# Seven idle products, an earlier load of the cap, and a layer norm shared out anew among three engines

## The chip, the core and the metric

The kernel runs on one NeuronCore of a Trainium2 chip. Five engines work side by side, each through its own queue in program order: TensorE (PE, with its weight loads PEld), VectorE (DVE), ScalarE (ACT), GpSimd (POOL), and SyncE (SP), which only issues transfers here. An instruction that waits holds up everything behind it on its engine. The metric is the device time of one execution in microseconds (us); the median of three runs is given, beside one execution that was profiled.

## What is computed

Attention with a capped score, then a Fourier mixing over tokens and features, a layer norm without weights, and a feed-forward block; four batches, 12 heads of 64, 448 tokens, all in f32:

```python
scores = cap * tanh((q @ k.T / 8) / cap)                 # cap is a scalar input, 30.0
attn = exp(scores - max); attn = attn / (sum(attn) + 1e-9)
x = (attn @ v) with the heads side by side               # (4, 448, 768)
u = x + real(fft(fft(x, axis=1), axis=2))
un = (u - mean(u)) / sqrt(var(u) + 1e-6)                 # over the 768 features
out = u + relu(un @ w_ch1) @ w_ch2                       # 768 -> 3072 -> 768
```

## The kernel before

**Stages.** Scores are made in tiles t = 0, 1, 2, ... of two heads and up to 128 keys: `scores` writes 2 x 450 columns to one of two PSUM buffers with four products, one for each quarter of the array (line 376). ScalarE turns them into `a` with tanh (386, scale `tscale`) and exp in place (389, scale `capt`). `weigh` multiplies them with v (405) into one PSUM buffer `av`, for a pair of heads, with a column of ones for the row sums. `denominators` (420, 421) adds `guard`, the place of 1e-9, and takes the reciprocal; `normalise` (427) writes the pair's part of `u` and so frees `av` for the next pair. When a batch has its six pairs, the mixing follows (446 to 529), then the norm.

**The norm of a batch b.** `moments` leaves mean and variance of every token in `stat`: 113 rows by 4 groups of tokens. `rows` makes scale and bias of every token from them, on GpSimd: ten operations on 128x4 values, among them a power of -0.5 (549) and one step of Newton's method to sharpen it. `rows_cols` (561) turns mean and deviation into two rows by a product with the identity, for a later addition; `rows_copy` (567) and `rows_out` bring them to memory. `standardise` (582) scales and shifts `u` in place, four operations of 113x768 on VectorE. `u_cols` (589) transposes the result, `u_copy` (297, as `xc<-pt`) fetches it from PSUM, `operand` and `operand_rest` split it into a high and a low part (`xs`, 297 and 302).

**Feed-forward.** The weights come as 64-bit numbers and are split by VectorE and ScalarE (`wt`, 636 to 670). `product` calls `up` (`ph`, 723; ScalarE's relu 734; VectorE's rest 735) and `down` (`po`, 752; VectorE's accumulation 761). The first products fill places between the attention and the norms; after about 260 us the products run in a row to the end.

**What sets the order.** Every step is a function that is put in a plan with `at(f, ...)`. Its place is a number from the table `ORDER`, one list per function; the plan is sorted by these numbers and run inside `tc.manual_schedule()`. The queues hold what a step issues, in that order but for small moves by the framework's scheduler, which puts an instruction where it reckons its inputs to be there.

**What the change touches.** `load_cap` and `scales` with their numbers in `ORDER`, the head of the program before the plan, `rows`, `rows_cols` and `standardise`.

Of the kernel before, what the change touches and what calls it, by code (L numbers as in the profile page):

```python
# [11 lines left out]
F32 = mybir.dt.float32  # L12
# [105 lines left out]
    "load_cap": [  # L118
        4
# [144 lines left out]
def attention_fft_ffn(  # L264
# [44 lines left out]
    nc.scalar.activation(guard, mhalf[:, :1], AF.Tanh)  # L309

# [8 lines left out]
    def load_cap():  # L319
        nc.sync.dma_start(capt, cap.partition_broadcast(P))  # L320

    def scales():
        nc.vector.reciprocal(tscale, capt)
        nc.vector.tensor_scalar_mul(tscale, tscale, 1.0 / math.sqrt(D))


        nc.vector.tensor_scalar_mul(ncap, capt, -1.0)
        nc.vector.tensor_tensor(ncap, ncap, capt, op=ALU.min)
        nc.scalar.activation(guard, ncap, AF.Exp)
        nc.vector.tensor_scalar_mul(guard, guard, 1e-9)  # L330
# [210 lines left out]
    def rows(b):  # L541


        ln = line[b] = new([P, 2, 4, 2], F32, "ln", 2, "ln")
        var = new([P, 4], F32, "var", 1, "var")
        t = new([P, 4], F32, "nt", 1, "nt")
        nc.gpsimd.tensor_copy(ln[:, 0, :, 0], stat[b][:, :, 0])
        nc.gpsimd.tensor_scalar_add(var, stat[b][:, :, 1], 1e-6)
        nc.gpsimd.tensor_tensor(ln[:, 1, :, 0], var, mhalf, op=ALU.pow)  # L549
        nc.gpsimd.tensor_tensor(t, ln[:, 1, :, 0], ln[:, 1, :, 0], op=mul)  # L550
        nc.gpsimd.tensor_tensor(t, t, var, op=mul)
        nc.gpsimd.tensor_scalar(t, t, -0.5, 1.5, op0=mul, op1=add)
        nc.gpsimd.tensor_tensor(ln[:, 1, :, 0], ln[:, 1, :, 0], t, op=mul)
        nc.gpsimd.tensor_tensor(ln[:, 0, :, 1], ln[:, 1, :, 0], var, op=mul)
        nc.gpsimd.tensor_tensor(t, ln[:, 0, :, 0], ln[:, 1, :, 0], op=mul)
        nc.gpsimd.tensor_scalar_mul(ln[:, 1, :, 1], t, -1.0)

    def rows_cols(b):
# [3 lines left out]
            ps[:8, :R], line[b][:R, 0].rearrange("q g a -> q (g a)"), ident[:R, :R], start=True, stop=True  # L562
# [16 lines left out]
    def standardise(b, g):  # L579
        u, ln = u_t[b][:R, g], line[b]  # L580
        scale, bias = ln[:R, 1, g, :1], ln[:R, 1, g, 1:]
        nc.vector.tensor_scalar(u, u, scale, bias, op0=mul, op1=add)
# [222 lines left out]
    at(load_cap)  # L805
    at(scales, needs=[("load_cap",)])
# [17 lines left out]
    def attend(t):  # L824
# [6 lines left out]
        for p in range(B * NP):  # L831
            if 7 * p + 6 in (2 * t, 2 * t + 1):
                at(denominators, p, needs=[("weigh", 7 * p + 6)] + ([("denominators", p - 1)] if p else []))
# [148 lines left out]
```

## Time and profile before

| | |
|---|---|
| median of 3 runs | 934.06 us (934.03 to 934.49) |
| the profiled execution | 935.5 us |
| its span, first to last instruction | 933.4 us |
| busy: PE, PEld | 914.4, 790.5 us (98%, 85%) |
| busy: DVE, ACT, POOL | 715.6, 325.9, 16.7 us (77%, 35%, 2%) |
| chain of waits, by engine | PE 86%, ACT 8%, DVE 3%, POOL 1%, issue 1% |

The profile is of one execution. The chain of waits follows the work that ended last back to what released it, step by step; idle time of an engine that is not on it costs nothing. Three quarters of it are the products of lines 723 and 752. The change stands in the first quarter of the span, so the rows that follow are of the start and of the four norms: GpSimd's rows of batches 0 to 3 begin at 84.8, 135.0, 189.1 and 231.6 us.

### The profile page before, as it was taken

How to read it: one execution, taken by the hardware profiler on the slowest of the kernel's cores; microseconds unless marked ns; L12 is line 12 of the kernel's file. 1: busy time of each engine (PE TensorE's matmuls, PEld its weight loads, DVE VectorE, ACT ScalarE, POOL GpSimd, SP SyncE). 2: the span in 40 equal slices, each digit the busy share in tenths (PEclk: the TensorE clock that was granted, in tenths of full speed). 3: DMA queues.
4: the chain of work that ended last, by engine and by line, in shares of the span. 5: the costliest groups of instructions: out<-in, count | busy, mean ns of one | idle time of the engine just before them, and what ended most of it. 6: DMA issues, size and time to landing. Idle time of an engine off the chain costs nothing.

```text
span 933.4 us, 18643 instructions
## 1 busy us (share of the span) xinstructions
PE 914.4 (98%) x7816; PEld 790.5 (85%) x7816; DVE 715.6 (77%) x1446; ACT 325.9 (35%) x499; POOL 16.7 (2%) x47
## 2 busy tenths in 40 slices
PE   7999999989999999999999999999999999999998
PEld 4666776668889999999998999999999999999997
DVE  2689798879989787878878778777787777778633
ACT  7989989851312222122121221222122221222200
POOL 0001010010100000000000000000000000000000
PEclk9999999989999999999999999999999999999999
DMA  6654435210203121221211121211222111221033
GB/s 184 170 154 136 129 90 129 65 38 1 79 0 85 52 61 51 61 65 54 61 51 61 52 64 47 60 51 51 54 55 63 51 51 51 53 67 51 18 119 118
DMA packets 50467, 66.63 MB, mean 71 GB/s; under 512 B 25552, under 2 KB 36560, under 8 KB 50384
## 3 DMA queue, kind: packets, MB, share of 16 engines
q1 hardware_dynamic: 50240, 65.22, 24.6%
q8 instruction: 61, 1.00, 0.4%
q10 hardware_dynamic: 144, 0.23, 0.1%
q14 instruction: 22, 0.18, 0.1%
HBM read 59.91 MB, written 5.52 MB: 70 GB/s over the span
## 4 chain that ended last, share of the span: by engine, by line
PE 86%; ACT 8%; DVE 3%; issue 1%; POOL 1%; DMA 0%; POOLq 0%; DVEq 0%
PE ph L723 37%; PE po L752 37%; PE av L405 5%; PE s L376 4%; ACT a L389 4%; ACT a L386 4%; PE yps L477 1%; PE pq L505 1%; PE pt L589 1%; DVE bs L538 0%; DMA q<-qr 0%; POOL ln L549 0%; DVE hh L735 0%; DVE xc L761 0%; DVE y L497 0%
## 5 line engine op out<-in xcount | busy, mean ns | idle before, releaser
L752 PE MATMUL po<-hh,w 128*128 128x448 f32 x1728 | 362.4, 367 | 2.0 <-DVE xc L761 1.6
L723 PE MATMUL ph<-xs,w 128*128 128x448 f32 x1728 | 360.1, 367 | 0.0
L752 PEld LDWEIGHTS po<-hh,w 128*128 128x128 f32 x1728 | 322.6, 188 | 34.2 <-DVE xc L761 4.5
L723 PEld LDWEIGHTS ph<-xs,w 128*128 128x128 f32 x1728 | 324.1, 188 | 28.6 <-issue 0.4
L761 DVE TENSOR_TENSOR xc<-xc,po 128x448 f32<-128x448 f32 x288 | 176.1, 617 | 43.0 <-PE po L752 42.7
L735 DVE SCALAR_TENSOR_TENSOR hh<-ph,hh 128x448 fp32r<-128x448 f32 x96 | 59.9, 624 | 97.0 <-ACT hh L734 96.9
L636 ACT ACTIVATE wt<-raw 128x384 f32<-128x384 f32 x84 | 46.6, 555 | 231.1 <-DVE w L670 231.1
L734 ACT ACTIVATE hh<-ph 128x448 fp32r<-128x448 f32 x96 | 52.3, 545 | 191.8 <-PE ph L723 191.8
L405 PEld LDWEIGHTS av<-vt,a 128*64 128x64 f32 (+3 forms) x3072 | 88.2, 133 | 30.1 <-issue 19.0
L405 PE MATMUL av<-vt,a 128*64 128x65 f32 (+3 forms) x3072 | 94.3, 225 | 4.3 <-issue 3.4
L389 ACT ACTIVATE a<-a,capt 128x900 f32<-128x900 f32 x84 | 85.3, 1043 | 1.4
L386 ACT ACTIVATE a<-s,tscale 128x900 f32<-128x900 f32 x84 | 82.5, 1002 | 9.5 <-PE s L376 9.1
L297 ACT CAST w<-wt 128x384 fp32r<-128x384 f32 x84 | 42.8, 510 | 119.2 <-DVE wt L645 119.2
L376 PE MATMUL s<-q,k 64*64 64x450 f32 x672 | 78.0, 563 | 5.9 <-DMA q<-qr 4.7
L645 DVE SCALAR_TENSOR_TENSOR wt<-wt 128x384 f32<-128x384 f32 x96 | 53.6, 559 | 9.5 <-DVE wt L642 0.5
L642 DVE SCALAR_TENSOR_TENSOR wt<-raw,wt 128x384 uint32<-128x384 uint32 x96 | 53.7, 559 | 3.3
L670 DVE TENSOR_TENSOR w<-wt 128x384 fp32r<-128x384 f32 x96 | 53.6, 558 | 3.3
L664 DVE SCALAR_TENSOR_TENSOR wt<-raw,wt 128x384 f32<-128x384 uint32 x96 | 53.5, 558 | 2.9
L302 DVE TENSOR_TENSOR wt<-wt,w 128x384 f32<-128x384 f32 x96 | 52.8, 550 | 0.0
L376 PEld LDWEIGHTS s<-q,k 64*64 64x64 f32 x672 | 20.2, 135 | 27.9 <-ACT a L386 12.1
L639 DVE TENSOR_SCALAR wt<-raw 128x384 uint32<-128x384 uint32 x96 | 34.1, 355 | 1.1
L661 DVE TENSOR_SCALAR wt<-wt 128x384 uint32<-128x384 uint32 x96 | 34.0, 354 | 0.6
(58 smaller groups left out, 323.9 us busy)
## 6 DMA issues: line engine op xcount, KB each, us to landing
raw<-w2r SPq DMA_DIRECT2D x48, 384.0 KB, 4.1
raw<-w1r SPq DMA_DIRECT2D x48, 384.0 KB, 3.0
q<-qr SPq DMA_DIRECT2D x35, 225.0 KB, 4.3
outT<-xc SPq DMA_DIRECT2D x24, 224.0 KB, 1.9
k<-kr SPq DMA_DIRECT2D x12, 256.0 KB, 3.5
vt<-vr SPq DMA_DIRECT2D x24, 128.0 KB, 4.5
k<-kr SPq DMA_DIRECT2D x12, 192.0 KB, 2.4
vt<-vr SPq DMA_DIRECT2D x24, 96.0 KB, 4.1
```

The source lines that it names most:

```text
L376: nc.tensor.matmul(ps_t[t][h * D : (h + 1) * D, n, :SQ], kt[q, k][rows, k0, h], qk[q, x][rows], start=True, stop=True,)
L386: nc.scalar.activation(a_t[t], ps_t.pop(t)[:, :, :SQ], AF.Tanh, scale=tscale)
L389: nc.scalar.activation(a_t[t], a_t[t], AF.Exp, scale=capt)
L405: nc.tensor.matmul(pa_t[p][q0:q1, j, g * (D + 1) : (g + 1) * (D + 1)], a_t[t][rows, n, OFF[g] + q0 : OFF[g] + q1], vt[rows, p % 2, i], sta ...
L642: nc.vector.scalar_tensor_tensor(tu, hi.bitcast(U32), 0xC0000000, tu, op0=ALU.bitwise_and, op1=ALU.bitwise_or)
L645: nc.vector.scalar_tensor_tensor(t, w, HI_MIN, t, op0=ALU.is_ge, op1=mul)
L664: nc.vector.scalar_tensor_tensor(w, lo, 2.0**-52, w, op0=mul, op1=mul)
L670: nc.vector.tensor_tensor(ws[c][1][:, sl], t, w, op=add)
L723: nc.tensor.matmul(ph[:, :S], w_[:, dc * P : (dc + 1) * P], x_, start=(k_ == 0), stop=(k_ == 3 * NDC - 1),)
L735: nc.vector.scalar_tensor_tensor(hh[:, 1], ph[:, :S], 0.0, f32(hh[:, 0]), op0=ALU.max, op1=sub)
L752: nc.tensor.matmul(po[:, :S], w_[:, dc * P : (dc + 1) * P], hh[:, x_], start=(k_ == 0), stop=(k_ == 3 * GF - 1),)
L761: nc.vector.tensor_tensor(ac, ac, po[:, :S], op=add)
```

## The change

- Ahead of the plan, in a scheduled block of its own, seven products of the identity with itself into a PSUM buffer that nobody reads, and behind them the load of the cap. `load_cap` is no longer a step.
- `scales` keeps the two operations for `tscale`. The four for `guard` (one of them an exp on ScalarE) are a step `guards`, number 13, which the denominators need.
- `rows`: GpSimd adds 1e-6 and takes the power. VectorE does six operations: three for Newton's factor, its product with the power, the bias in one operation from mean and scale, and the deviation, which is written over the variance in `stat`. The copy of the mean is gone, and `rows_cols` reads `stat`.
- `standardise`: for the last batch, b = 3, on ScalarE (`Identity` with scale and bias); the others stay on VectorE.

```diff
-    "load_cap": [
-        4
+    "guards": [
+        13
...
+    with tc.manual_schedule():
+        warm = psum.tile([P, 512], F32, tag="d", name="warm")
+        for _ in range(7):
+            nc.tensor.matmul(warm[:, :P], ident, ident, start=True, stop=True)
+        nc.sync.dma_start(capt, cap.partition_broadcast(P))
...
     def scales():
         nc.vector.reciprocal(tscale, capt)
         nc.vector.tensor_scalar_mul(tscale, tscale, 1.0 / math.sqrt(D))
+
+    def guards():
         nc.vector.tensor_scalar_mul(ncap, capt, -1.0)
...
-        nc.gpsimd.tensor_copy(ln[:, 0, :, 0], stat[b][:, :, 0])
-        nc.gpsimd.tensor_scalar_add(var, stat[b][:, :, 1], 1e-6)
-        nc.gpsimd.tensor_tensor(ln[:, 1, :, 0], var, mhalf, op=ALU.pow)
-        nc.gpsimd.tensor_tensor(t, ln[:, 1, :, 0], ln[:, 1, :, 0], op=mul)
-        nc.gpsimd.tensor_tensor(t, t, var, op=mul)
-        nc.gpsimd.tensor_scalar(t, t, -0.5, 1.5, op0=mul, op1=add)
-        nc.gpsimd.tensor_tensor(ln[:, 1, :, 0], ln[:, 1, :, 0], t, op=mul)
-        nc.gpsimd.tensor_tensor(ln[:, 0, :, 1], ln[:, 1, :, 0], var, op=mul)
-        nc.gpsimd.tensor_tensor(t, ln[:, 0, :, 0], ln[:, 1, :, 0], op=mul)
-        nc.gpsimd.tensor_scalar_mul(ln[:, 1, :, 1], t, -1.0)
+        mean, var, r = stat[b][:, :, 0], stat[b][:, :, 1], ln[:, :, 0]
+        nc.gpsimd.tensor_scalar_add(t, var, 1e-6)
+        nc.gpsimd.tensor_tensor(r, t, mhalf, op=ALU.pow)
+        nc.vector.tensor_tensor(n, t, r, op=mul)
+        nc.vector.tensor_tensor(n, n, r, op=mul)
+        nc.vector.tensor_scalar(n, n, -0.5, 1.5, op0=mul, op1=add)
+        nc.vector.tensor_tensor(r, r, n, op=mul)
+        nc.vector.scalar_tensor_tensor(ln[:, :, 1], mean, -1.0, r, op0=mul, op1=mul)
+        nc.vector.tensor_tensor(var, t, r, op=mul)
...
-            ps[:8, :R], line[b][:R, 0].rearrange("q g a -> q (g a)"), ident[:R, :R], start=True, stop=True
+            ps[:8, :R], stat[b][:R].rearrange("q g a -> q (g a)"), ident[:R, :R], start=True, stop=True
...
-        nc.vector.tensor_scalar(u, u, scale, bias, op0=mul, op1=add)
+        if b == B - 1:
+            nc.scalar.activation(u, u, AF.Identity, bias=bias, scale=scale)
+        else:
+            nc.vector.tensor_scalar(u, u, scale, bias, op0=mul, op1=add)
```

Three places show what became of it in the built programs. TensorE at the head of the program (`s` are the score products, four to a tile; the semaphores that a row waits for stand in brackets), before:

```order
L376 MATMUL s<-q,k 64x450 [waits DMAHW1_49,DMAHW0_49]
L376 MATMUL s<-q,k 64x450 x7
L376 MATMUL s<-q,k 64x450 [waits Activation_49]
L376 MATMUL s<-q,k 64x450 x3
L376 MATMUL s<-q,k 64x450 [waits Activation_49]
L376 MATMUL s<-q,k 64x450 [waits DMAHW3_49]
L376 MATMUL s<-q,k 64x450
```

and now:

```order
L380 MATMUL s<-q,k 64x450 [waits DMAHW2_49,DMAHW0_49]
L380 MATMUL s<-q,k 64x450 x7
L380 MATMUL s<-q,k 64x450 [waits Activation_49]
L380 MATMUL s<-q,k 64x450 x2
L313 MATMUL warm<-ident 128x128 [waits Pool_49]
L313 MATMUL warm<-ident 128x128 x6
L380 MATMUL s<-q,k 64x450
L380 MATMUL s<-q,k 64x450 [waits Activation_49]
L380 MATMUL s<-q,k 64x450 [waits DMAHW3_49]
L380 MATMUL s<-q,k 64x450
L380 MATMUL s<-q,k 64x450 [waits DMAHW5_49]
```

The seven products stand behind tiles 0 and 1 and three products of tile 2, not at the head.

VectorE at the norm of batch 1 (`wt` and `w` are the split weights, `den` the denominators), before:

```order
L664 SCALAR_TENSOR_TENSOR wt<-raw,wt 128x384
L582 TENSOR_SCALAR u<-u,ln 113x768 x4
L302 TENSOR_TENSOR xs<-xc,xs 128x448
L420 TENSOR_SCALAR den<-av,guard 113x8
L421 RECIPROCAL den<-den 113x8
L567 COPY rowt<-rt 8x113
L427 TENSOR_TENSOR u<-av,den 113x4x128
```

and now:

```order
L668 SCALAR_TENSOR_TENSOR wt<-raw,wt 128x384
L552 TENSOR_TENSOR var<-nt,ln 128x4
L553 TENSOR_TENSOR var<-var,ln 128x4
L554 TENSOR_SCALAR var<-var 128x4
L555 TENSOR_TENSOR ln<-ln,var 128x4
L556 SCALAR_TENSOR_TENSOR ln<-stat,ln 128x4
L557 TENSOR_TENSOR stat<-nt,ln 128x4
L586 TENSOR_SCALAR u<-u,ln 113x768 x4
L302 TENSOR_TENSOR xs<-xc,xs 128x448
L424 TENSOR_SCALAR den<-av,guard 113x8
L425 RECIPROCAL den<-den 113x8
L568 COPY rowt<-rt 8x113
```

The six operations stand ahead of the standardising and of the next pair's denominators.

ScalarE at the norm of batch 3 (`hh` is the relu, `xs` a cast, `xc` a copy from PSUM), before:

```order
L297 COPY xc<-pt 128x448 [waits PE_49]
L734 ACTIVATE hh<-ph 128x448 [waits PE_49]
L297 CAST xs<-xc 128x448 [waits DMAHW0_49]
L297 COPY xc<-pt 128x448
L734 ACTIVATE hh<-ph 128x448 [waits PE_49]
L297 COPY xc<-pt 128x448 [waits PE_49] x5
```

and now:

```order
L297 COPY xc<-pt 128x448 [waits PE_49]
L738 ACTIVATE hh<-ph 128x448 [waits PE_49]
L584 ACTIVATE u<-u,ln 113x768 [waits DVE_49]
L584 ACTIVATE u<-u,ln 113x768
L297 CAST xs<-xc 128x448 [waits DMAHW0_49]
L297 COPY xc<-pt 128x448
L584 ACTIVATE u<-u,ln 113x768 x2
L738 ACTIVATE hh<-ph 128x448 [waits PE_49]
```

The four standardisings stand in two pairs around a cast and a copy, and ahead of the second relu.

## Rows read from the trace of the kernel before

**Rows 1.** The page: busy time of each engine, share, instructions.

```profile
PE 914.4 (98%) x7816; PEld 790.5 (85%) x7816; DVE 715.6 (77%) x1446; ACT 325.9 (35%) x499; POOL 16.7 (2%) x47
```

**Rows 2.** Timeline at the start: start, length, engine, line, work, count, [idle before].

```profile
1.17 0.42 SPq L320 DMA_DIRECT2D capt<-cap  x1
...
6.66 0.20 ACT L329 ACTIVATE guard<-ncap 128x1 f32<-128x1 f32 x1 [4.00 <-DVE ncap L328]
6.76 0.99 ACT L386 ACTIVATE a<-s,tscale 128x900 f32<-128x900 f32 x1
...
8.01 1.01 ACT L386 ACTIVATE a<-s,tscale 128x900 f32<-128x900 f32 x1 [0.25 <-PE s L376]
...
12.04 0.99 PE L376 MATMUL s<-q,k 64*64 64x450 f32 x8
12.78 1.89 ACT L386 ACTIVATE a<-s,tscale 128x900 f32<-128x900 f32 x2
...
17.28 2.92 ACT L389 ACTIVATE a<-a,capt 128x900 f32<-128x900 f32 x3
```

**Rows 3.** The chain of waits: start, share of the chain, work, records.

```profile
4.67 3.32 PE s L376 x16
...
66.36 1.72 PE s L376 x16
...
106.64 0.94 PE pt L589 x8
...
142.34 0.29 PE rt L561 x2
```

**Rows 4.** Timeline at batch 0's norm, VectorE and TensorE.

```profile
90.34 0.69 DVE L427 TENSOR_TENSOR u<-av,den 113x512 f32<-113x512 f32 x1
...
92.47 0.64 PE L405 MATMUL av<-vt,a 64*64 64x65 f32 x32
```

**Rows 5.** Timeline at batch 1's norm, VectorE and TensorE.

```profile
138.31 0.55 DVE L664 SCALAR_TENSOR_TENSOR wt<-raw,wt 128x384 f32<-128x384 uint32 x1
139.44 2.45 DVE L582 TENSOR_SCALAR u<-u,ln 113x768 f32<-113x768 f32 x4 [0.58 <-POOL ln L556]
...
142.34 0.22 DVE L420 TENSOR_SCALAR den<-av,guard 113x8 f32<-113x8 f32 x1
142.59 0.20 DVE L421 RECIPROCAL den<-den 113x8 f32<-113x8 f32 x1
...
142.99 0.67 DVE L427 TENSOR_TENSOR u<-av,den 113x512 f32<-113x512 f32 x1
...
143.90 0.64 PE L405 MATMUL av<-vt,a 64*64 64x65 f32 x32
```

**Rows 6.** Timeline at batch 2's norm; last a stretch with its granted clock (0.50).

```profile
190.20 1.39 POOL L549 TENSOR_TENSOR ln<-var,mhalf 128x4 f32<-128x4 f32 x1
...
193.90 1.27 DVE L582 TENSOR_SCALAR u<-u,ln 113x768 f32<-113x768 f32 x2 [1.41 <-POOL ln L556]
...
196.18 0.69 DVE L427 TENSOR_TENSOR u<-av,den 113x512 f32<-113x512 f32 x1
...
188.13 3.63 PE L405 MATMUL av<-vt,a 128*64 128x65 f32 x128
...
196.97 6.23 PE L405 MATMUL av<-vt,a 64*64 64x65 f32 x128 [3.17 <-issue]
...
196.97:202.70 5.73, 5.73 (x118) 0.50 0.26 72
```

**Rows 7.** Timeline at batch 3's norm, VectorE, TensorE and ScalarE.

```profile
237.08 1.84 DVE L582 TENSOR_SCALAR u<-u,ln 113x768 f32<-113x768 f32 x3
...
238.42 1.27 PE L589 MATMUL pt<-ident,u 113*128 113x113 f32 x8
...
244.57 1.50 PE L752 MATMUL po<-hh,w 128*128 128x448 f32 x6 [0.74 <-DVE xc L761]
...
246.50 1.50 ACT L297 CAST xs<-xc 128x448 fp32r<-128x448 f32 x3 [2.73 <-PE pt L589]
```

More of the change, by code (lines that the diff above doesn't have):

```diff
@@ L309, in attention_fft_ffn @@
     nc.scalar.activation(guard, mhalf[:, :1], AF.Tanh)
+    with tc.manual_schedule():
[3 more added lines that the diff above has]
+        nc.sync.dma_start(capt, cap.partition_broadcast(P))
     vt = new([P, 2, NC, D + 1], F32, "vt", 1, "vt")
     nc.gpsimd.memset(vt[:, :, :, D:], 1.0)
-    def load_cap():
-        nc.sync.dma_start(capt, cap.partition_broadcast(P))
     def scales():
@@ L541, in rows @@
     def rows(b):
-        ln = line[b] = new([P, 2, 4, 2], F32, "ln", 2, "ln")
-        var = new([P, 4], F32, "var", 1, "var")
+        ln = line[b] = new([P, 4, 2], F32, "ln", 2, "ln")
         t = new([P, 4], F32, "nt", 1, "nt")
-        nc.gpsimd.tensor_copy(ln[:, 0, :, 0], stat[b][:, :, 0])
-        nc.gpsimd.tensor_scalar_add(var, stat[b][:, :, 1], 1e-6)
-        nc.gpsimd.tensor_tensor(ln[:, 1, :, 0], var, mhalf, op=ALU.pow)
-        nc.gpsimd.tensor_tensor(t, ln[:, 1, :, 0], ln[:, 1, :, 0], op=mul)
-        nc.gpsimd.tensor_tensor(t, t, var, op=mul)
-        nc.gpsimd.tensor_scalar(t, t, -0.5, 1.5, op0=mul, op1=add)
-        nc.gpsimd.tensor_tensor(ln[:, 1, :, 0], ln[:, 1, :, 0], t, op=mul)
-        nc.gpsimd.tensor_tensor(ln[:, 0, :, 1], ln[:, 1, :, 0], var, op=mul)
-        nc.gpsimd.tensor_tensor(t, ln[:, 0, :, 0], ln[:, 1, :, 0], op=mul)
-        nc.gpsimd.tensor_scalar_mul(ln[:, 1, :, 1], t, -1.0)
+        n = new([P, 4], F32, "var", 1, "var")
+        mean, var, r = stat[b][:, :, 0], stat[b][:, :, 1], ln[:, :, 0]
[7 more added lines that the diff above has]
+        nc.vector.tensor_tensor(var, t, r, op=mul)
     def rows_cols(b):
@@ L580, in standardise @@
         u, ln = u_t[b][:R, g], line[b]
-        scale, bias = ln[:R, 1, g, :1], ln[:R, 1, g, 1:]
-        nc.vector.tensor_scalar(u, u, scale, bias, op0=mul, op1=add)
+        scale, bias = ln[:R, g, :1], ln[:R, g, 1:]
+        if b == B - 1:
+            nc.scalar.activation(u, u, AF.Identity, bias=bias, scale=scale)
+        else:
+            nc.vector.tensor_scalar(u, u, scale, bias, op0=mul, op1=add)
     def u_cols(b, p):
@@ L803, in convert @@
                 at(weights, 3 * i + n, needs=[("fetch", i)] + ([("weights", 3 * i + n - 1)] if i + n else []))
-    at(load_cap)
-    at(scales, needs=[("load_cap",)])
+    at(scales)
+    at(guards, needs=[("scales",)])
     for i in range(4):
@@ L832, in attend @@
             if 7 * p + 6 in (2 * t, 2 * t + 1):
-                at(denominators, p, needs=[("weigh", 7 * p + 6)] + ([("denominators", p - 1)] if p else []))
+                at(denominators, p, needs=[("weigh", 7 * p + 6), ("guards",)] + ([("denominators", p - 1)] if p else []))
                 at(normalise, p, needs=[("denominators", p)])
```

## The prediction

> **What bounds the kernel now.** I read the page first: TensorE is busy for 98% of the span [rows 1], so a gain has to come from places where it stands or runs slowly, and any work added to it counts unless it falls into a wait. The chain of waits then says where those places are. From 282 us on it is feed-forward products back to back, and the change touches nothing there. Before that there are two kinds of stretch. At the start the first two tiles of scores (16 records) take 3.32 us, where two later tiles take 1.72 [rows 3], and from 8.9 to 60.8 us the chain is ScalarE alone, tanh and exp in turn. From 104 us it is mostly TensorE. Next I read the timelines engine by engine around the four layer norms, batches 0 to 3. In batch 2 TensorE stands for 3.17 us before the weighing at 196.97, which then runs at a granted clock of 0.50 (1.2 instead of 2.4 GHz), so that it takes 6.23 us where a full one took 3.63 [rows 6]. In batch 3 it waits 0.74 us for VectorE at 244.57 [rows 7].
>
> **The idle products.** The text of the change puts them first; the built program does not. In TensorE's order they stand behind eleven score products, after the third of tile 2's four. So they run near 8.8 us, with work behind them, and nothing at the head of the program becomes quicker. Seven products are 14 records, as one f32 product is two (the rt row). A record of like shape costs 0.94/8 = 0.12 (transposes) to 0.29/2 = 0.145 us (rt) [rows 3]: 1.7 to 2.0, and I take 1.7, the transposes' rate in a row of many. A tile's four products run side by side, two tiles costing 1.72 [rows 3]. Cut into three and one, a tile needs up to 0.86 more, or less if the fourth runs beside tile 3: 0 to 0.9, I take 0.75. Against this, tile 3 may not start before tanh 1 ends at 9.02 [rows 2], while tile 2, released by tanh 0 at 7.76, is done near 8.65: 0.35 us of wait are swallowed. TensorE is late by 1.7 + 0.75 - 0.35 = 2.1 at tile 4, which ends at 13.03 now and 15.1 then. Its tanh is the second of the pair at 12.78, starting near 13.7 [rows 2]. ScalarE is thus held by 15.15 - 13.7 = **1.4 us**, and since the chain is ScalarE from there to 60.8, it keeps that. Bounds: 0.4 (products at half that price, no cost of the cut) to 2.2 (both upper prices, no wait swallowed).
>
> **The cap first, the guard later.** SyncE issues the cap ahead of k, so k moves back by one issue, 0.42 us [rows 2]; it lands beside q, and the first product needs both: 0 to 0.42, I take 0.2. The scales come that much earlier, which helps nobody: tanh 1 waited 0.25 us for its products, not for the scales. The guard's exp leaves the place before tanh 0 (6.66, 0.1 us ahead of it [rows 2]), where that wait hid it, and stands between tanh 1 and the first exp, where nothing hides it: +0.1. Both lie inside the 1.4, because tanh 4 then waits for TensorE anyway; alone they would cost 0.3. The only reader of the guard is the first denominators, microseconds later.
>
> **The row operations.** GpSimd keeps two of ten, VectorE gets six (the copy and a scaling vanish). On VectorE an operation on a few columns takes 0.25 and 0.20 us from start to start [rows 5], so six cost 1.2 to 1.5; I take 1.25. They stand in VectorE's queue, with the denominators and the normalising of a later pair queued behind; the next weighing needs the one PSUM buffer that this normalising frees.
> Batch 0: normalising ends at 91.03 and would end at 92.28; the next weighing starts at 92.47 [rows 4]: hidden, **0**, up to 0.25 if the cover is 0.2 less. VectorE has 2 us of idle behind it.
> Batch 1: VectorE is free at 138.86; today it waits for GpSimd and standardises from 139.44. Then it starts at 138.86 + 1.25 = 140.11, 0.67 later; normalising ends at 144.33 instead of 143.66, and the weighing of 143.90 starts near 144.4 [rows 5]: **+0.5** (0 to 0.8).
> Batch 2: VectorE idles 1.41 us for GpSimd today [rows 6]. Without the copy ahead, the power ends near 191.1 instead of 191.59, and VectorE, free at 190.7, waits 0.4 for it. Then 0.4 + 1.25 stand where 1.41 stood: normalising, which ends at 196.87 and releases the weighing at 196.97, moves by **+0.2** (-0.3 to +0.5). What is late next is the same VectorE queue, so TensorE's stall stays.
>
> **Batch 3 on ScalarE.** The last of VectorE's four standardisings ends at 238.92 and the transposes at 238.42 to 239.7 wait for it [rows 7]. On ScalarE no row shows one. The nearest are exp, 900 columns from SBUF, 2.92/3 = 0.97 [rows 2], and the cast, 448 columns, 1.50/3 = 0.50 [rows 7]; 768 columns lie between, at 0.50 + 0.47 x 320/452 = 0.83, nearer to exp, which like these takes an operand from a tile. I take 0.85. The rows on VectorE follow its weight work that ends at 235.0, so they end at about 236.05 for the scale and bias; ScalarE's order is two standardisings, a cast and a copy (0.93 together), two more: 236.05 + 4 x 0.85 + 0.93 = 240.4. That is 1.5 us later for TensorE. It also waits 0.7 us for the rt product before that, inside the same delay. VectorE loses 2.4 us of standardising and gains 1.25, so it is ready for its accumulation when TensorE gets there, and the 0.74 us wait at 244.57 goes: 1.5 - 0.74 = **+0.75**. Bounds: at 0.5 a piece +0 (a gain would need the 0.74 to go without the transposes being late), at 0.97 +1.3.
> The Trainium skill (ScalarE: Activation LUTs, What ACT_TABLE_LOAD costs) gives 186 ns + 0.833 ns per column, 93 ns for each operand that is a pointer, 93 ns of overlap: 0.92 us here in a row, two pointers; exp's rows bear it out (1.03 by the rule). The whole sum by it would be 937.2, an estimate from that page.
>
> **Sum.** 1.4 + 0 + 0.5 + 0.2 + 0.75 = 2.85 us. The profiled execution has a span of 933.4 and a time of 935.5 us, 1.4 above the median of the runs, 934.06; the sum is a difference, so the span would be 936.25 and the median 934.06 + 2.85 = **936.9**.
>
> **Rivals.**
> A: the clock. The stall of batch 2 comes some 2 us later after a different run of work, and the fall to 0.50 might be shorter or not come. Whole price 6.23 - 3.63 = 2.6 [rows 6]: 936.9 - 2.6 = 934.3, not slower than before; it decides from the point where less than 1.0 of the 2.6 is left. For it: the wait was broken by one short product only, so it may be a close call. Against: the stall is as long as before.
> B: the idle products are hidden. ScalarE has 0.7 us of slack at tile 4; if products and cut cost 1.1, only 0.4 is kept: 935.9.
> C: the change does what it says, the products first. Then the first two tiles cost 1.72 instead of 3.32 and ScalarE starts about 1.1 earlier: 934.06 - 1.1 + 1.45 = 934.4. The order speaks against it flatly.
> D: batch 3 gains. If ScalarE's standardisings were done by 239, the 0.74 would be a gain: 935.4; together with A 932.8.
> E: the slow clock of the start lasts through the idle products and doubles their price: about 939.
>
> **How the numbers follow.** Forecast 0.57 (935.6 to 938.3 by the bounds of its terms), A 0.20, B 0.07, C 0.02, D 0.08, E 0.06. The measurement can tell about 0.2%, 1.87 us, from no change: "same" is 932.2 to 935.9. A, B, C and most of D fall there, with the lower end of the forecast; a little of D with A lies below. Faster 0.06, same 0.32, slower 0.62. The range reaches to A and stops short of E: 934.0 to 938.5.
>
> **What would show it.** The seven products near 8.8 us, about 1.7 us long, and tile 4's tanh near 15.1; if they stand before 4.7, C holds. Exp and tanh at 60 us some 1.4 later than today. VectorE's six operations at 0.2 each; the weighing of batch 1 waiting for normalising, about half a microsecond. In batch 2 a stall of about 3 us before the weighing, and its clock: 0.50 again, or A. In batch 3 the last standardising near 240.4 plus 2.1, four of about 0.9, and no wait at the later accumulation. The forecast is wrong if TensorE's queue regains the 2 us before 60, or if the stall of batch 2 shrinks.

## The result, and the profile of the changed kernel

The changed kernel takes 939.62 us (median of 4 runs, 939.5 to 940.79), the kernel before 934.27 us in the same comparison (4 runs, 934.03 to 934.69). The ratio is 1.0055 with a 95% interval of 1.0042 to 1.0067: slower by 5.35 us. The forecast was 936.9, with a range from 934.0 to 938.5. The direction was right, the size was not, and the time lies above the range.

The page of the changed kernel (span 937.8, time 939.54 us) shows TensorE still at 98%, against [rows 1], with 14 products more, and the chain's shares hardly moved:

```profile
PE 916.8 (98%) x7830; PEld 792.9 (85%) x7830; DVE 716.1 (76%) x1466; ACT 330.2 (35%) x503; POOL 6.4 (1%) x15
...
PE 86%; ACT 10%; DVE 2%; issue 1%; DMA 0%; SPq 0%; ACTq 0%
```

**The start.** The chain of waits of the changed kernel (start, share of the chain, work, records):

```profile
0.72 0.39 SPq L314
...
1.17 4.44 DMA k<-kr
...
5.75 4.50 PE s L380 x22
10.25 1.76 PE warm L313 x14
12.01 1.65 PE s L380 x10
13.66 2.01 PE av L409 x63
15.67 0.96 PE s L380 x8
...
16.65 1.01 ACT a L390
```

The chain begins with the issue of the cap (L314), and k, issued behind it, is what the first score product waits for. It starts at 5.75 us, where it started at 4.67 [rows 3]. The seven products (`warm`) take 1.76. The tanh of tile 4 starts at 16.65; before, it was the second of the pair at 12.78 [rows 2], at 13.69. So ScalarE is 2.96 us late there, 1.08 of it by k.

**Batch 1 and behind it**, from the timeline (start, length, engine, line, work, count, [idle before]):

```profile
141.86 0.55 DVE L668 SCALAR_TENSOR_TENSOR wt<-raw,wt 128x384 f32<-128x384 uint32 x1
142.33 0.16 DVE L552 TENSOR_TENSOR var<-nt,ln 128x4 f32<-128x4 f32 x1
...
143.32 2.45 DVE L586 TENSOR_SCALAR u<-u,ln 113x768 f32<-113x768 f32 x4
...
147.64 0.69 PE L409 MATMUL av<-vt,a 64*64 64x65 f32 x32
...
153.80 0.98 PE L380 MATMUL s<-q,k 64*64 64x450 f32 x8 [1.07 <-ACT a L393]
```

VectorE's six operations take 1.0 us, and the weighing of 143.90 [rows 5] starts at 147.64, 3.74 late. VectorE's weight work just ahead of the norm, 138.31 in [rows 5] and 141.86 here, was 3.55 late: the norm of batch 1 costs 0.2. At 153.80 a score tile waits 1.07 us. No such wait stood in the kernel before. The profile puts it down to an exp; the experiments say something else.

**Batches 2 and 3**, timeline of TensorE:

```profile
201.08 5.11 PE L409 MATMUL av<-vt,a 64*64 64x65 f32 x128 [3.64 <-issue]
...
239.04 0.36 PE L562 MATMUL rt<-ident,stat 113*8 113x113 f32 x2 [0.46 <-DVE stat L557]
...
242.77 0.42 PE L593 MATMUL pt<-ident,u 112*128 112x112 f32 x2 [0.61 <-ACT u L584]
243.69 0.71 PE L593 MATMUL pt<-ident,u 112*128 112x112 f32 x5 [0.50 <-ACT u L584]
...
245.50 2.59 PE L756 MATMUL po<-hh,w 128*128 128x448 f32 x6
```

and two stretches with their granted clock (from and to, length, busy time and count by engine, then PEclk):

```profile
core 0: us, PE busy (x) PEld busy (x) DVE busy (x) ACT busy (x) POOL busy (x), PEclk, DMA share, GB/s
...
201.00:204.50 3.50, 3.42 (x76) 3.33 (x78) 1.86 (x4) 0.00 (x0) 0.00 (x0) 0.51 0.18 28
...
245.40:248.70 3.30, 3.30 (x14) 2.93 (x13) 2.50 (x6) 0.94 (x2) 0.00 (x0) 0.50 0.42 105
```

In batch 2 the stall before the weighing is 3.64 us, and the stretch at 0.50 (1.2 GHz) behind it is over at 204.4, so that the weighing takes 5.11 instead of 6.23 [rows 6]. In batch 3 TensorE waits for the row product and twice for ScalarE, and then runs at 0.50 a second time, at 245.4, where the kernel before ran at full clock.

### The profile page after: what moved, and what is told of

It is laid out like the page before. It is cut to its first block, busy times and chain, and to the rows that moved or that the text cites. A ratio compares the mean times of both kernels' runs of the same rounds, so it can differ in the third digit from the quotient of the medians.

```text
span 937.8 us, 18663 instructions
## 1 busy us (share of the span) xinstructions
PE 916.8 (98%) x7830; PEld 792.9 (85%) x7830; DVE 716.1 (76%) x1466; ACT 330.2 (35%) x503; POOL 6.4 (1%) x15
## 3 DMA queue, kind: packets, MB, share of 16 engines
q8 instruction: 62, 1.02, 0.4%
## 4 chain that ended last, share of the span: by engine, by line
PE 86%; ACT 10%; DVE 2%; issue 1%; DMA 0%; SPq 0%; ACTq 0%
PE po L756 37%; PE ph L727 37%; PE av L409 5%; PE s L380 4%; ACT a L393 4%; ACT a L390 4%; PE pq L509 1%; PE yps L481 1%; PE pt L593 1%; DMA k<-kr 0%; ACT u L584 0%; DVE xc L765 0%; DVE bs L542 0%; ACT xc L297 0%; ACT xs L297 0%
## 5 line engine op out<-in xcount | busy, mean ns | idle before, releaser
L409 PE MATMUL av<-vt,a 128*49 128x65 f32 (+3 forms) x3072 | 92.9, 224 | 4.6 <-issue 3.9
```

The lines of the kernel that those rows point to most:

```text
L409: nc.tensor.matmul(pa_t[p][q0:q1, j, g * (D + 1) : (g + 1) * (D + 1)], a_t[t][rows, n, OFF[g] + q0 : OFF[g] + q1], vt[rows, p % 2, i], sta ...
```

## The experiments

Ratios are against the kernel before in the same comparison, with 95% intervals; one per mille is 0.94 us.

| kernel | median us | of before | ratio |
|---|---|---|---|
| changed | 939.62 | 934.27 | 1.0055 (1.0042 to 1.0067) |
| `u_cap`: changed, k ahead of the cap again | 939.42 | 935.04 | 1.0051 (1.0038 to 1.0064) |
| `u_idle`: changed, no idle products | 936.22 | 935.04 | 1.0013 (1.0005 to 1.0022) |
| `u_start`: new norm alone | 935.02 | 935.04 | 1.0001 (0.9992 to 1.0010) |
| `u_norm`: new start alone | 939.56 | 935.04 | 1.0053 (1.0040 to 1.0066) |
| `before_again`: before, unchanged | 934.86 (one run) | 935.01 | |
| `i_wide`: changed, 2 wide idle products for 7 | 938.09 | 935.01 | 1.0031 (1.0019 to 1.0043) |
| `i_first`: changed, 7 idle products really first | 937.76 | 935.01 | 1.0033 (1.0020 to 1.0045) |
| `best`: before, 2 wide idle products first | 935.26 | 935.01 | 1.0001 (0.9992 to 1.0009) |
| `b_seven`: before, 7 idle products first | 935.50 | 935.34 | 1.0003 (0.9995 to 1.0012) |
| `b_fourteen`: before, 14 narrow ones first | 940.19 | 935.34 | 1.0057 (1.0044 to 1.0070) |
| `r_only`: before, new row operations alone | 934.15 | 935.34 | 0.9987 (0.9979 to 0.9996) |
| `b_std`: before, batch 3 on ScalarE alone | 937.56 | 935.34 | 1.0022 (1.0013 to 1.0030) |
| `b_cap`: before, cap first alone | 936.22 | 935.08 | 1.0012 (1.0004 to 1.0021) |
| `b_idle`: before, 7 idle products alone | 938.07 | 935.08 | 1.0033 (1.0021 to 1.0046) |
| `r_wide`: `r_only` and `best` together | 934.23 | 935.08 | 0.9992 (0.9983 to 1.0001) |

### Start or norm: one part undone

`u_cap` puts the load of the cap back behind that of k:

```diff
-        nc.sync.dma_start(capt, cap.partition_broadcast(P))
...
+    at(load_cap)
+    at(scales, needs=[("load_cap",)])
```

> The changed kernel with one part undone: the load of the cap stands behind that of k again; the seven products, the later guard and the norm stay as changed. Theory (queue): the cap's small packets hold the queue that k shares, so k lands late and everything after it is late by the 1.08 us that the first score product is later in the trace (5.75 against 4.67). Expected: first product at 4.67, the lag of ScalarE's chain at 60 us 1.9 instead of 3.0, a median near 938.5. Rival (the prediction's own term): k moves by 0.2 and that lies inside the idle products' 1.4, so undoing it changes 0 to 0.2 us, a median of 939.4 to 939.6.

`u_idle` takes the products out:

```diff
-        for _ in range(7):
-            nc.tensor.matmul(warm[:, :P], ident, ident, start=True, stop=True)
```

> The changed kernel without the seven idle products; the cap stays ahead of k, guard and norm as changed. Theory: the products cost what the trace has in a row, 1.76 us, and about 1.9 with the cut of tile 2; without them the lag at 60 us is 1.1 (the cap alone) and the median near 937.7. Rival (the prediction's term): 1.4 less, a median of 938.2, since 0.5 of the products would be swallowed by ScalarE's slack at tile 4. Second rival: a later clock for the first tiles without the products gives part back, a median over 938.5.

`u_start` undoes both and the later guard; `u_norm` has the norm's three functions of the kernel before instead:

```diff
 # u_start: the edits of u_cap and u_idle, and
-    def guards():
-    at(guards, needs=[("scales",)])
 # u_norm: rows, rows_cols and standardise as before
-        nc.vector.tensor_tensor(n, t, r, op=mul)
...
+        nc.gpsimd.tensor_scalar_mul(ln[:, 1, :, 1], t, -1.0)
...
-            nc.scalar.activation(u, u, AF.Identity, bias=bias, scale=scale)
```

> All of the start undone (no idle products, k ahead of the cap, the guard early): the new norm alone. Theory: no lag before 85 us, then the norm's own cost as the changed kernel's trace has it: +0.25 in batch 1, batch 2 between -0.5 and +0.2, batch 3 about +2 with a fall of the granted clock to 0.50 after TensorE's waits for ScalarE: +2.3 in all, a median near 936.6. Rival (time decides, not work): the shorter slow stretch of batch 2 and the new one of batch 3 came from the 3 us of shift; with the start undone batch 3 keeps full clock, and batch 2's slow stretch is 6.8 us again: +1.0 to +1.4, a median of 935.2.

> The norm undone (rows on GpSimd, all standardising on VectorE), the changed start kept. Theory: the whole lag of 3.0 us at 60 us stays to the end, and batch 3 has no slow stretch: a median near 937.1 to 937.3. Rival (the prediction): the start costs 1.4, a median of 935.5. Second rival (time decides): the shift of the start alone brings a slow stretch in batch 3, a median over 938.5.

The norm alone costs 0.1 us, not the 2.3 that I had read from the changed kernel's trace, and the start alone costs all of it (1.0053 against 1.0055). None of my four expectations came true, and three (`u_idle`, `u_start`, `u_norm`) fell on the same error: I had taken what lies behind 85 us for the norm's. The rival of `u_norm` has the time right but not the cause, as its profile has no second stretch at 0.50. Without the products 4 per mille go, twice what they take at their place. `u_cap` gained 0.4 of the 1.1 us expected, which is nearer to its rival (0 to 0.2); the intervals of the two ratios overlap, so that pair does not decide the cap's price (`b_cap`, below, does).

### What the products cost away from their place

`before_again` is the kernel before, unchanged. `i_wide` has the 896 idle columns in two products, `i_first` reads zeros that VectorE sets instead of the identity, `best` has two wide products on such zeros and nothing else:

```diff
 # i_wide
-        for _ in range(7):
-            nc.tensor.matmul(warm[:, :P], ident, ident, start=True, stop=True)
+        for n in (3, 4):
+            nc.tensor.matmul(warm[:, : n * P].rearrange("p (n c) -> p n c", n=n),
+                ident, ident[:, None, :].to_broadcast([P, n, P]), start=True, stop=True)
 # i_first
+    zero = keep.tile([P, P], F32, name="zero")
+    nc.vector.memset(zero, 0.0)
-            nc.tensor.matmul(warm[:, :P], ident, ident, start=True, stop=True)
+            nc.tensor.matmul(warm[:, :P], zero, zero, start=True, stop=True)
 # best: zero as in i_first, the two products as in i_wide, on the kernel before
+                zero, zero[:, None, :].to_broadcast([P, n, P]), start=True, stop=True)
```

> The kernel before, unchanged, for a second profile. Its first one had a time of 935.5 us with one slow stretch of 6.8 us. Theory: that profile is on the slow side of its own spread; another one has a span nearer to 932 to 933 and differs from it in the length of the slow stretch of batch 2 and in a drift of under 1 us over the feed-forward, not in the order or size of any wait before 190 us (all starts there within 0.2 us). Rival: the waits at 96 and 149 us vary by a microsecond from one execution to the next of the same kernel, in which case differences between kernels there mean nothing.

> The changed kernel with the 896 idle columns in two products (384 and 512) instead of seven of 128, at the same place of TensorE's program: 8 instructions (four weight loads, four matmul passes) where there were 28, for the same columns. Theory (instruction stream): the wait of 1.07 us at 152.7 stands at a fixed number in TensorE's stream (its 6276th instruction in three kernels with the seven products, while the kernels without them have none there); with 20 instructions fewer ahead of it, another product stands at that number and the wait shrinks below 0.4 us, with the lag at 60 us as before (2.7 to 3.0): a median of 938.6 to 939.2. Rival (ScalarE): the wait there comes from ScalarE's copy being 0.26 late for the transposes; the lag is the same, so the wait stays near 1 us, a median of 939.6.

> The changed kernel with the seven products reading a tile that VectorE sets to zero in place of the identity that GpSimd makes: in TensorE's order they then stand first, ahead of all score products. All else as changed, the cap ahead of k too. Theory: they run from about 1.1 to 4.6 us at the slow clock, under the wait for k; the clock rises before the scores begin at 5.75, the first two tiles take 1.72 instead of 3.3, and ScalarE, at 60 us, is 0 to 0.3 late against the kernel before instead of 3.0; with the stream's 28 instructions and the norm still in it a median of 935.8 to 937.0. Rival: the clock falls back in the wait between 4.6 and 5.75 us, so that the first tiles take 3.3 again: lag 1.1 at 60 us, a median near 937.5. Second rival: the products end after 5.75 and delay the scores: over 938.

> The kernel before with only one thing added: two idle products (384 and 512 columns of zeros set by VectorE) first in TensorE's program; k stays ahead of the cap, guard and norm as before. Theory: they lie under the wait for q and k, the clock is up at 4.7 us, two tiles take 1.72 instead of 3.32 and ScalarE's chain starts about 1.1 earlier and keeps it to 60 us; if nothing gives it back, 1 us under the kernel before, a ratio of 0.999. Rival (given back): the earlier chain meets the loads and the norms' waits, so that at 200 us nothing is left: a ratio of 1.000. Second rival: eight instructions more shift the stream so that a new wait of about 1 us appears: a ratio of 1.000 to 1.001.

`before_again` told two things. In its timeline a weighing near 97 us waits 1.03 us for nothing that the profile shows; in the first profile of the same kernel that wait was 0.2. And its stretch at 0.50 in batch 2 ends 3.4 us after it began, not 6.8 (stretches in the second fence):

```profile
97.46 0.80 PE L405 MATMUL av<-vt,a 128*49 128x65 f32 x21 [1.03 <-issue]
```

```profile
197.40:200.70 3.30, 2.90 (x66) 2.81 (x68) 2.18 (x5) 0.00 (x0) 0.00 (x0) 0.50 0.08 7
200.80:204.00 3.20, 3.20 (x77) 3.10 (x74) 1.12 (x3) 0.67 (x2) 0.00 (x0) 1.00 0.33 113
```

So the expectation that all starts before 190 us agree within 0.2 fell: one wait there varies by 0.8 from one execution to the next. And a shorter stretch in one profile of the changed kernel shows nothing by itself. The profiles together show more: the stretch is 3.4 us long in all eight with the new row operations; of the nine with the old ones, four have 3.4 and five 6.8.

In `i_first` the products do stand first, and end before k lands; the timelines of TensorE in `i_first` and in `best`:

```profile
1.07 3.35 PE L315 MATMUL warm<-zero 128*128 128x128 f32 x14 [1.07 <-DVE zero L311]
5.74 4.09 PE L382 MATMUL s<-q,k 64*64 64x450 f32 x24 [1.32 <-DMA k<-kr]
```

```profile
1.07 3.36 PE L315 MATMUL warm<-zero 128*128 128x384 f32 x4 [1.07 <-DVE zero L311]
4.54 1.94 PE L385 MATMUL s<-q,k 64*64 64x450 f32 x16
```

With k ahead of the cap (`best`) two tiles follow at once in 1.94 us instead of 3.32 [rows 3]. With the cap ahead there are 1.32 us of wait between, and the tiles are as slow as without the products: the first rival of that run. At 60 us `i_first` is level with `u_idle`, which has no products (ScalarE's timelines of the one and the other):

```profile
61.88 0.99 ACT L392 ACTIVATE a<-s,tscale 128x900 f32<-128x900 f32 x1
```

```profile
61.87 0.99 ACT L387 ACTIVATE a<-s,tscale 128x900 f32<-128x900 f32 x1
```

and still it ends at 1.0033 against 1.0013, 1.9 us later. Whatever costs this comes after 60 us, and comes from products that were over at 4.4 us. It is not the second stretch at 0.50 in batch 3, which `i_first`'s profile has and `u_idle`'s has not: the three runs of each with a mean granted clock of 0.998 take 937.4 and 935.1 us. What `i_first`'s profile has besides, and `u_idle`'s has not, is a wait near 152 us as in the changed kernel:

```profile
153.42 0.98 PE L382 MATMUL s<-q,k 64*64 64x450 f32 x8 [1.78 <-ACT a L392]
```

`best` is 0.6 to 0.8 us early at 60 us (60.14 for a tanh that starts at 60.70 and 60.91 in two profiles of the kernel before), and nothing of it is left at the end: its first rival. `i_wide`, with the same columns at the old place but 20 instructions fewer, is 2.3 us under the changed kernel by the ratios (the intervals just touch), where I had expected 0.4 to 1.0; its wait near 152 us is gone, and another has come near 160.

### A wait that stands at a number

The stretch view counts instructions. From 0 to the end of each wait of which the profile names no good releaser it gives TensorE's products and weight loads; their sum is the number in its stream at which it stood. Changed kernel, `before_again`, `i_wide`:

```profile
0.00:99.56 99.56, 92.08 (x1997) 60.65 (x1998) 63.69 (x155) 85.21 (x93) 2.01 (x9) 1.00 0.55 155
0.00:153.79 153.79, 145.15 (x3138) 97.79 (x3138) 109.83 (x264) 135.17 (x155) 3.39 (x11) 1.00 0.50 140
```

```profile
0.00:97.46 97.46, 90.09 (x1997) 58.84 (x1998) 63.20 (x149) 86.17 (x94) 4.75 (x17) 1.00 0.57 159
```

```profile
0.00:160.84 160.84, 151.17 (x3265) 101.29 (x3265) 114.38 (x270) 141.45 (x162) 3.40 (x11) 1.00 0.51 140
```

The wait near 97 to 99 us stands at 1997 + 1998 = 3995 in both kernels, although the changed one has 28 instructions more ahead of it and so another product there. The wait of 153.80 stands at 6276, as in `u_cap`, `u_norm`, `i_first` and `b_idle`; that of `i_wide` at 6530, 254 further. From 3995 to 6276 it is 2281, nine times 253.4. Two more kernels ask whether the number or the work decides: the kernel before with 7 products of 128 columns first (28 instructions), and with 14 of 64 (56).

```diff
+    zero = keep.tile([P, P], F32, name="zero")
+    nc.vector.memset(zero, 0.0)
+    with tc.manual_schedule():
+        warm = psum.tile([P, 512], F32, tag="d", name="warm")
+        for _ in range(14):     # b_seven: range(7), 128 columns
+            nc.tensor.matmul(warm[:, :64], zero, zero[:, :64], start=True, stop=True)
```

> The kernel before with seven idle products of 128 columns, on a tile of zeros set by VectorE, first in TensorE's program: the columns and the place of the two wide products whose kernel came out level with the one before (1.0001), but 28 instructions in place of 8. Theory (instruction stream): the start gains as much as with the two wide ones, and the 20 instructions more bring a wait of 0.7 to 1.9 us before the score tile near 150 us, at TensorE's 6276th instruction, and put the one of the tile near 90 us at its 3742nd: a ratio of 1.0010 to 1.0025. Rival: how many instructions the idle work takes is indifferent; what costs is that the products were in the way: a ratio of 1.0000 to 1.0005 and no wait near 150 us.

> As the seven, with the same columns in fourteen products of 64: 56 instructions. Theory (instruction stream): TensorE's 6276th instruction is then one of the weighing ahead of the score tiles near 150 us; the wait stands there, inside a run of weighing products, at the same number, 1 to 2 us long; the product that stood at 6276 with seven has none. The time is some ratio from 1.0005 to 1.0030; the place is what the run tells. Rival: waits there belong to the work (the score tile that waits for ScalarE), so a wait stands before the same score tile as with seven, at number 6304, or nowhere.

`b_seven`, its wait and the count up to it:

```profile
148.82 0.98 PE L382 MATMUL s<-q,k 64*64 64x450 f32 x8 [0.62 <-issue]
```

```profile
0.00:148.81 148.81, 144.16 (x3138) 98.22 (x3138) 108.06 (x251) 134.41 (x155) 8.48 (x27) 1.00 0.52 144
```

`b_fourteen`:

```profile
153.49 0.37 PE L411 MATMUL av<-vt,a 128*49 128x65 f32 x5 [1.51 <-issue]
```

```profile
0.00:92.99 92.99, 89.19 (x1871) 60.88 (x1871) 58.04 (x139) 79.63 (x87) 4.74 (x17) 1.00 0.56 155
...
0.00:153.49 153.49, 147.38 (x3139) 101.62 (x3139) 107.74 (x249) 134.50 (x154) 8.48 (x27) 1.00 0.52 140
```

With 28 instructions the wait is at 6276, before the second score tile; with 56 at 6278, in the middle of a run of weighing products that wait for nobody, and the score tiles behind it have none. It stands at a number, whatever work is there. The place was as expected. The price was not: `b_seven` is only 0.2 us over `best`, where I had expected 1 to 2. In its profile the wait at 3995 was 0.28 and the one at 6276 was 0.62, together 0.9; `best` has one wait, of 0.87 at 3995. The same sum is 0.73 in `u_idle` and 1.09 + 1.78 in `i_first`, 2.1 more. So the sum of these waits, and not the new one alone, tells what a shift costs. It varies by execution, and for `i_wide` against the changed kernel it does not tell the difference of the medians: `i_wide`'s profile, the slowest of its six runs, has 1.14 + 1.20 and the changed kernel's 0.28 + 1.07. And `b_fourteen`'s time is not the waits' alone, since 28 narrow records take as long each as wide ones: in its trace they run to 7.3 us and the scores start 2.4 us late.

What stands at these numbers is the loading of TensorE's own instructions. The page of the changed kernel counts the loads of one queue (packets, MB, share):

```profile
q8 instruction: 62, 1.02, 0.4%
```

That is 16 KB each, and one for every 253 of TensorE's 15660 products and weight loads; VectorE has 1466 instructions in all. When TensorE goes on at number 3995, 6276 or 6530, the 15th, the 24th or the 25th of these loads has just landed: in the traces of all kernels such a wait ends 1.3 to 1.6 us after the load's last byte. In the changed kernel's transfers there is no instruction load between 144 and 151.2 us, while data fill two thirds of the engines' time, and one (0.02 MB) between 151.2 and 153.8, which the wait ends:

```profile
q1 hardware_dynamic: 1358, 1.11, 67.5%
```

```profile
q1 hardware_dynamic: 739, 0.24, 47.9%
q8 instruction: 1, 0.02, 2.3%
```

The Trainium skill (Runtime: NRT & Kernel Launch, Instruction fetch mechanics) says that an engine's instructions are loaded in blocks of 16 KiB, which are 256, while it runs, and that crossing from one into the next is mostly hidden. The trace agrees with the block: the waits lie 253 (3742 and 3995) and 254 (6276 and 6530) products and weight loads apart, and instructions of other kinds are not in these counts. With "mostly hidden" it disagrees at these places, at 0.2 to 1.8 us each. That the block came late because of the q, k and v loads in the same stretch is only argued; no run took those loads away. For it speaks `i_wide`, where the data fill 78% of the engines' time from 153 to 158.5 us without an instruction load, and 5% from there to 160.8; the load starts at 158.60:

```profile
q1 hardware_dynamic: 21, 0.03, 5.0%
q8 instruction: 1, 0.02, 2.4%
```

### The norm's two halves

`r_only` has the new `rows` and `rows_cols`, all else as before; `b_std` only this:

```diff
+        if b == B - 1:
+            nc.scalar.activation(u, u, AF.Identity, bias=bias, scale=scale)
+        else:
+            nc.vector.tensor_scalar(u, u, scale, bias, op0=mul, op1=add)
-        nc.vector.tensor_scalar(u, u, scale, bias, op0=mul, op1=add)
```

> The kernel before with the new row operations alone (two on GpSimd, six on VectorE, the rows' product from stat); batch 3 is standardised on VectorE, and the start is undone. Theory: batch 0 hidden, batch 1 +0.2, batch 2 -0.5 to 0 since TensorE's wait for the row product and for the weighing together shrink from 4.1 to 3.64 us, batch 3 +0.2 (VectorE standardises that much later) with the later wait of 0.74 left: a ratio of 0.9995 to 1.0002. Rival (the prediction's terms): +0.5 and +0.2 and +0.2, a ratio of 1.0010.

> The kernel before with the last batch standardised on ScalarE and nothing else changed; the rows stay on GpSimd. Theory: four operations of 1.02 us and ScalarE's copy and cast between them end 2.0 us later than VectorE's four, TensorE waits twice for them (0.6 and 0.5), and the later wait of 0.74 for VectorE goes: +0.4 to +0.9 in batch 3, a ratio of 1.0004 to 1.0010, or up to 1.0025 where the granted clock falls after these waits. Rival: the waits are all inside the 0.74 that goes, a ratio of 0.9998 to 1.0002.

The row operations alone make the kernel faster, 0.9987, below what I had expected for the run: one half of the change, which the prediction had charged with 0.7 us (0.5 and 0.2), is a gain. TensorE in batch 2, `before_again` and then `r_only`:

```profile
194.27 0.36 PE L561 MATMUL rt<-ident,ln 113*8 113x113 f32 x2 [0.94 <-POOL ln L554]
197.80 1.44 PE L405 MATMUL av<-vt,a 64*64 64x65 f32 x34 [3.17 <-issue]
```

```profile
193.12 0.36 PE L557 MATMUL rt<-ident,stat 113*8 113x113 f32 x2
197.12 1.06 PE L404 MATMUL av<-vt,a 64*64 64x65 f32 x40 [3.64 <-issue]
```

The row product no longer waits for GpSimd, and 0.94 + 3.17 = 4.11 us of waiting become 3.64. That is 0.5 of the 1.2 us by the ratio. Another 0.5 is the stretch at 0.50 behind this weighing. The record has the mean granted clock of every run: 0.996 in the profiles with 6.8 us of such stretches, 0.998 in those with 3.4. Of the kernel before, 15 of the 29 runs have 0.996 and take 935.8 us on average, the others 934.7; of `r_only`'s 11 runs one has 0.996, and the others take 934.0. At a like clock 0.7 us is gained, and the rest because the longer stretch has become rare. `b_std` costs 2.1 us. Its TensorE in batch 3, and the stretch behind:

```profile
240.63 0.41 PE L592 MATMUL pt<-ident,u 112*128 112x112 f32 x2 [1.50 <-ACT u L583]
241.55 0.71 PE L592 MATMUL pt<-ident,u 112*128 112x112 f32 x5 [0.51 <-ACT u L583]
```

```profile
243.10:246.40 3.30, 3.30 (x13) 2.93 (x13) 2.31 (x7) 1.07 (x2) 0.00 (x0) 0.50 0.33 86
```

The waits, and after them a granted clock of 0.50 as in the changed kernel's batch 3. The upper end of the expectation, with the clock, held. Together the halves give 0.1 (`u_start`), less than 2.1 - 1.2 = 0.9: with the new rows ScalarE gets scale and bias earlier, and TensorE's wait for it is 0.65 in that trace where it is 1.50 here. The intervals allow either.

```profile
238.95 0.42 PE L588 MATMUL pt<-ident,u 112*128 112x112 f32 x2 [0.65 <-ACT u L579]
239.87 0.71 PE L588 MATMUL pt<-ident,u 112*128 112x112 f32 x5 [0.50 <-ACT u L579]
```

Behind these two waits in `u_start`'s profile the clock stays at 1.00 from 239.9 to 244.0 us, and so it does in `u_idle`'s profile behind 0.65 and 0.50; in the changed kernel it falls behind 0.61 and 0.50. So the second stretch does not follow from these waits alone. What else it takes stays open. `u_start` is `r_only` with batch 3 on ScalarE: with the new rows that step costs 0.1 + 1.2 = 1.3 us by the ratios.

### Each part of the start alone

`b_cap` and `b_idle` add one part of the start to the kernel before; `r_wide` joins the edits of `r_only` and `best`, the two that lost nothing.

```diff
 # b_cap
-    at(load_cap)
+    with tc.manual_schedule():
+        nc.sync.dma_start(capt, cap.partition_broadcast(P))
 # b_idle
+    with tc.manual_schedule():
+        warm = psum.tile([P, 512], F32, tag="d", name="warm")
+        for _ in range(7):
+            nc.tensor.matmul(warm[:, :P], ident, ident, start=True, stop=True)
```

> The kernel before with the load of the cap ahead of that of k, and nothing else changed. Theory (queue): k's packets go behind the cap's 128 in the queue of SyncE; the first score product starts at 5.7 instead of 4.7 to 4.8, ScalarE's chain is 0.9 to 1.1 late at 60 us, and the end as well: a ratio of 1.0008 to 1.0015. Rival (the prediction's term): 0.2 us, a ratio of 1.0002, as the changed kernel with k put first again (0.4 under the changed kernel in the ratios) would also let one think.

> The kernel before with the seven products on the identity alone; they come to stand where the changed kernel has them, behind eleven score products. Theory: 1.8 to 2.0 us at the place, and 28 instructions in the stream, with waits of 0.3 at the 3742nd and about 1 us at the 6276th instruction: a ratio of 1.003 to 1.0045. Rival (the prediction's term): 1.4 us in all, a ratio of 1.0015.

> The two parts that lost nothing together: the new row operations alone (ratio 0.9987 by themselves) and two wide idle products on zeros first in TensorE's program (1.0001 by themselves). Theory: the start gains 0.5 to 0.9 us at ScalarE, which the waits at fixed numbers of the stream give back near 96 us: a ratio of 0.9982 to 0.9990, no better than the rows alone. Rival: with the rows no longer late the start's gain reaches the end: 0.9975 to 0.9980.

The cap alone costs 1.1 us, as the theory had it. The transfers between 1.6 and 3.4 us show why; first `before_again`, then `b_cap` (packets, MB, share):

```profile
q1 hardware_dynamic: 108, 0.21, 49.4%
```

```profile
q1 hardware_dynamic: 104, 0.00, 2.9%
```

In the same 1.8 us the queue that k and the cap share carries 0.21 MB in the one kernel, and 104 packets with next to no bytes in the other. The cap is 4 bytes for each of 128 partitions: tiny to move, but k stands behind its packets. The first of k's packets of 2048 bytes starts at 1.75 us in `before_again`; in `b_cap` the cap's packets start at 1.73 and k's first at 3.29. The idle products alone cost 3.1 us, as expected, 1.9 at their place (in `b_idle`'s timeline tile 4's tanh starts at 15.70, against 13.69 in the kernel before and 13.82 in `u_start`) and the rest behind. The waits behind came out otherwise than expected: none at 3742, 1.38 at 3995 and 0.34 at 6276. `r_wide` came out at 0.9992, a little over its theory and no better than the rows alone.

## Why the prediction was wrong

**The sum.** Alone, the cap costs 1.1, the products 3.1 and the norm 0.1 us; that makes 4.3, and the whole 5.1 by its ratio, inside its interval. The forecast had 1.4 for the start and 1.45 for the norm. The start was short by 2.8 us, the norm too high by 1.35: its row operations gain 1.2 where the terms had +0.7, and batch 3 costs 1.3 where they had 0.75. The start in one kernel (`u_norm`) costs 5.0, 0.8 more than its two parts alone; the intervals are too wide to say whether that is real.

Two steps failed, the cap's term and the products' reach behind their place; the 1.35 in the norm hid part of it.

**The cap: the first step that failed.** "It lands beside q, and the first product needs both: 0 to 0.42, I take 0.2", inside the 1.4 of the products. I moved k by the time of one issue on SyncE. What moved it was the packets in the queue: 1.08 in the profile, 1.1 alone, two and a half times the upper bound, and not inside anything, since k is what the chain begins with.

**The idle products: right place, right length, and the second step that failed.** They cost 3.1 us alone, where I had 1.4. They stood behind eleven score products and took 1.76 us (1.7 forecast). At their place they cost 1.8 to 2.0 instead of 1.4: tile 2's own tanh waits 0.89 us for its fourth product, which I had not followed. What no term held, and so put at nothing, is that 28 instructions more move every product behind them past the fixed numbers of the instruction stream. What the products cost behind their place is some 1.2 us alone, and 1.9 between `u_idle` and `i_first`, though only 0.2 between `best` and `b_seven`. In the last two pairs the profiles' waits at the fixed numbers tell it, 2.1 and 0.0; that all of the 1.2 is theirs is not shown. The lower bound of 0.4 was wrong from the start: half price, no cut and 0.35 swallowed leave 0.5 us at tile 4, less than ScalarE's slack of 0.7 there, so 0.

**The guard.** +0.1, inside the rest: its exp stands between tanh 1 and the first exp, 0.19 long, and the tanh of tile 2 behind them waits for TensorE anyway. Not tested alone; without the products (`u_idle`) the first exp starts 1.00 us after tanh 1, where it is 0.91 in `u_start`, which has the guard early: 0.09.

**Batch 0** (0) and **batch 1** (+0.5, measured 0.2, in the range) held. **Batch 2** was +0.2 (-0.3 to +0.5); TensorE's two waits became 0.5 shorter, and the slow stretch behind them was short in every profile with the new rows. I had followed VectorE's queue alone and left out that the row product would no longer wait for GpSimd.

**Batch 3.** The mechanism held: two standardisings, a wait, two more, and the 0.74 at 244.57 [rows 7] gone. The term that was mis-sized is the length of one, from the source view of line 584 (shortest, median and longest in ns):

```profile
L584 ACT ACTIVATE u<-u,ln x4: 1017/1025/1029, 239.0 to 242.6; 113x768 f32<-113x768 f32 x4
```

1.02 instead of 0.85; in a row, two take 1.95. The rule of the Trainium skill (ScalarE: Activation LUTs, What ACT_TABLE_LOAD costs) gave 0.92 in a row and 1.01 for one; the trace agrees better with it than with my row between exp and cast. Not forecast at all was the second stretch at 0.50, which the changed kernel's profile has behind these waits.

**The rivals.** A (the stretch of batch 2 shorter) came true in part. The kernel before has both lengths, 6.8 and 3.4 us, in two profiles, so the one trace of the changed kernel proves nothing; but with the new rows all eight profiles have the short one, and `r_only`'s runs bear it out. It is worth some 0.5 us, not 2.6, and is in the gain of `r_only`. B and C fell: nothing hid the products, and they stood where the order said. C's premise was tested with zeros in place of the identity: two wide products first bring the two tiles to 1.94 us, and the end gains nothing (1.0001); nor does it with the seven (1.0003). D fell. E forecast the right time, about 939, by a mechanism that is not there: 14 records in 1.76 us are at full speed, since at the head of `i_first` the same 14 take 3.35. It was close: the trace's first record of the granted clock, at 1.00, is from 9.85 us, 0.4 ahead of them.

**A faster version** is `r_only`, the new row operations without the rest: 934.15 against 935.34 us, 0.9987 (0.9979 to 0.9996), below both kernels: a gain of 1.2 us.

## What to carry to other kernels

Ahead of a transfer count the packets in its queue, not only the issues: here a broadcast of 4 bytes to 128 partitions held a load of 256 KB back by a microsecond. Instructions added to a full engine can cost more than their time, since they shift all later ones against the block boundaries of the instruction stream: 1.9 us in one pair of kernels here, 0.2 in another. Two wide idle products in place of seven narrow ones were 2.3 us better in the changed kernel, by a cause that is not shown, and no better first in the program (1.0001 and 1.0003). A wait for which the profile names an unlikely releaser, or none, should be counted: if it stands at the same number in two kernels with different work, it belongs to the stream.

## What was not expected of the hardware

- TensorE waited at its 3994th or 3995th product or weight load in every kernel, 0.2 us in one profile of the kernel before, 1.03 in another and 1.38 in `b_idle`; at the 6276th only in kernels with 28 or 56 instructions more ahead.
- An f32 product of 64 columns first in the program costs nearly as much as one of 128: in `b_fourteen` 28 records took 6.23 us (0.22 each), in `i_first` 14 of 128 columns 3.35 (0.24).
- The first two tiles behind idle products ran at nearly full speed in `best`, where they followed at once (16 records in 1.94 us), and in `b_seven` after a wait of 0.41 us (16 in 1.74). They ran slowly in `i_first` after a wait of 1.32 us (24 in 4.09), but also in `b_fourteen`, where they followed at once (24 in 4.14); so the wait alone does not decide it.
